# Attention and a gated feed-forward layer on one core: the output products of the last two token blocks in Strassen's form

## The chip, the core and the metric

The kernel runs on one core of a Trainium2 chip. The core has five engines that run side by side, each through its own queue in order: PE (TensorE, the matmuls; its weight loads are shown apart as PEld), DVE (VectorE), ACT (ScalarE), POOL (GpSimd) and SP (SyncE, here only a DMA queue). Matmuls write to PSUM, eight banks of 128 partitions x 512 float32; DVE and ACT read it. The metric is the device time of one execution in microseconds (us), the median of several runs.

## The reference

```
scores = q @ k.T / 8 + bias[bucket(|i - j|), head]     # 8 sequences, 8 heads, 576 tokens, 64 wide
attn   = softmax(scores)
x      = (attn @ v), heads side by side                # 4608 tokens x 512
h      = x @ w_in                                      # 512 -> 2048
g      = h + sin(alpha * h)^2 / (alpha + 1e-9)
out    = g @ w_out                                     # 2048 -> 512, float32
```

The part that is changed is the last line, for 1024 of the 4608 tokens.

## The kernel before

All matmuls take float16 operands and add up in float32. The 4608 tokens are nine blocks of 512 (b = 0 to 8); the eight sequences of 576 tokens are stages t = 0 to 7. A stage has an exp phase (scores of sequence t, their exponentials on ACT, multiplication with the exponential of the bias on DVE near the diagonal, products with V on PE, normalisation on DVE), and then a sin phase: the input products of token block t, `plan_moe_in`, for 16 groups f of 128 hidden columns: four matmuls of 512 tokens into one of six PSUM banks ("h", banks 0 to 5), sin on ACT, the square on ACT or DVE, and the g of that group on DVE, which reads the bank a last time and frees it. The last stage, t = 7, has two blocks in its sin phase, 7 and 8. ACT changes its function table between the two phases.

The output products of block b, `plan_mo`, are four row blocks of 128 tokens (a = 0 to 3). Each is 16 matmuls, one per group f, with 128 tokens of g as weights and 512 columns of `w_out16` streaming, into one bank ("mo", banks 7 and 6); then a copy to SBUF by ACT or DVE, and one DMA of 128 x 512 float32 on the SP queue. The last row block, (8, 3), is cut in 384 and 128 columns. Output matmuls are marked `fill`: they are worked off wherever PE would have to wait, those of block t mostly in the exp phase of stage t + 1. Those of blocks 7 and 8 come after the input products of block 8, but for a few that fill in before.

The order of each engine's queue is made by a planner in the kernel (`Plan.run`) before anything is built: every step is a task with engines and estimated durations, what it depends on, a priority, and the buffers and banks that it takes; the planner puts the tasks on a simulated clock, always the one that can start first, by priority among those. That order is then written out, with semaphores. What an engine finds in its queue is therefore fixed: a step that waits holds up all that stands behind it.

Names that matter below: `gdone[(b, f)]` is the task that makes g of group f; `mo_last` chains all output matmuls in one sequence; `new_u()` and `new_outs()` take the next buffer of rings of two and five; a helper records every matmul, so all of them have one line (L458 before the change, L459 after it), and so have the plain copies (L538 on ACT, L540 on DVE). L1083 is g, L1069 the sin, L1076 and L1078 the square on ACT and DVE, L739 the bias multiplication, L708 the exponential, L953 and L954 the normalisation, L1141 the output DMA.

The heart of an output row block before:

```
for f in range(NF):
    full(m.v[:, 0 : c1 - c0], gcell[b].v[:, f, 128 * a : 128 * a + 128],
         w_out16[:, f, c0:c1], f == 0, f == NF - 1)
copy_on(e, o, m.v[:, 0 : c1 - c0])
nc.sync.dma_start(out=out[r0 : r0 + 128, c0:c1], in_=o)
```

Of the kernel before, what the change touches and what calls it, by code (L numbers as in the profile page):

```python
# [10 lines left out]
F16 = mybir.dt.float16  # L11
F32 = mybir.dt.float32
AF = mybir.ActivationFunctionType
ALU = mybir.AluOpType
# [6 lines left out]
def t_pe(n):  # L21
    return n / 2400.0 + 0.0025


def t_act(n):
    return n / 1200.0 + 0.052


def t_dve(n):
    return n / 960.0 + 0.07  # L30
# [4 lines left out]
LAT = {"PE": 0.2, "ACT": 0.18, "DVE": 0.18, "POOL": 0.2, "SP": 2.4}  # L35
NBUF = {"ut": 2, "u": 2, "g": 2, "s16": 3, "sq": 3, "outs": 5, "xn": 6}
PAIRS = ((0, 1), (2, 3), (4, 5))
BANKS = {"h": (0, 1, 2, 3, 4, 5), "av": (6, 7), "mo": (7, 6)}


class Task:
# [212 lines left out]
CP_PRI = 0  # L254
# [16 lines left out]
def kernel(  # L271
# [74 lines left out]


    xT = sgl.tile([128, NP, XN], F16, name="xT")


    natx = tp.tile([128, NF * DM], F16, name="natx", tag="g", bufs=2)
# [13 lines left out]
    def new_u():  # L365
        return tp.tile([128, 2, 9, 512], F16, name="u", tag="u", bufs=NBUF["u"])
# [18 lines left out]
    def bank(b, n=1):  # L385
        k = b.banks[0]
        return pb[:, k, :] if n == 1 else pb[:, k : k + n, :]
# [66 lines left out]
        eng.memset(vhs[i][64:128, :, VC + D : VC + D + 1], 1.0)  # L454
        eng.memset(vs[i][:, :, :, D : D + 1], 1.0)

    def full(out, lhsT, rhs, start, stop):
        nc.tensor.matmul(out=out, lhsT=lhsT, rhs=rhs, start=start, stop=stop)  # L458

    def warm(n, k=7):  # L460
        for _ in range(n):
# [74 lines left out]
    def copy_on(e, o, i):  # L536
        if e == "ACT":
            nc.scalar.activation(out=o, in_=i, func=AF.Copy)  # L538
        else:
            k_of(e).tensor_copy(out=o, in_=i)  # L540
# [263 lines left out]
    def plan_att(t, gates, gate):  # L804

        us = [(Cell(), Buf("u")) for _ in range(2)]
        tb, done = Buf("ut"), {}
        tails[t] = tb, done
        A = [(p, "A", c) for p in range(NP) for c in range(4)]
        runs = (A[0:3], [(0, "C", 0)], A[3:6], A[6:9], A[9:12], [(2, "C", 0)], A[12:15],  # L810
                A[15:] + [(0, "B", 0), (2, "B", 0)], [(0, "X", 0)])
        bases = [PB + 700 * i for i in range(len(runs))]
        exps, head, seen = [], [], set()
        for i, units in enumerate(runs):
            base = bases[i]
            made, deps, new, use = [], list(gates), [], []
            fresh = []
            for k, (p, kind, c) in enumerate(units):
                g = p // 2
                u, ub = us[g] if kind in "AC" else (None, tb)  # L820
                if ub not in new + use:
                    if ub in seen:
                        use.append(ub)
                    else:
                        new.append(ub)
                        seen.add(ub)
                        if u:
                            fresh.append(u)
                made.append(plan_unit(t, p, kind, c, u, ub, done, gate, base + 30 * k))
                if t < 2:  # L830
                    for pp in {"A": (p,), "C": (p, p + 1), "B": (p, p + 1), "X": range(NP)}[kind]:
                        deps += tr[(t, pp, 0)][1 if kind in "CX" else 0] + tr[(t, pp, 1)][0]
            tl = plan_tail(t - 1, base) if i == 0 and t > 1 else None

            def run(e, i=i, made=made, tl=tl, fresh=fresh):
                if i == 0:
                    plan.in_qk, plan.used = True, 0
                    plan.quota = QUOTA1 if t == 1 else QUOTA
                for u in fresh:
# [14 lines left out]
            m.offs = ([d] if tl else []) + [0.0] * len(new) + [  # L854
                0.1 + 0.2185 * k - GUARD[x[1]] * (k > 1) for k, x in enumerate(units)]
            m.marks = [(x[1], o) for x, o in zip(made, ends)] + ([(tl[4], d + D_TAIL)] if tl else [])
            head = [m]
            exps += [x[3] for x in made]
        for p in range(NP):
            plan_av(t, [(p, 128 * i) for i in range(3)], *us[p // 2], done, bases[(2, 3, 5, 7)[p]],  # L860
                    p < (2, NP - 1)[t > 1])
        for g in range(2):
            ps = [[2 * g, 2 * g + 1]] if g == 0 or t > 1 else [[2], [3]]
            for x in ps:
                plan_av(t, [(p, 384) for p in x], *us[g], done,
                        bases[(4, 7)[g]] + 50 if g == 0 or t == 1 else PB + AV_LATE, g == 0 or t > 1)
        return exps
# [248 lines left out]
    def plan_mo(b, a):  # L1116

        for c0, c1 in ((0, 384), (384, DM)) if (b, a) == (T, 3) else ((0, DM),):
            mb, ob, m = Buf("mo"), Buf("outs"), Cell()
            n = c1 - c0  # L1120
            for f in range(NF):

                def mm(e, f=f, m=m, mb=mb, c0=c0, c1=c1):
                    if f == 0:
                        m.v = bank(mb)
                    full(
                        m.v[:, 0 : c1 - c0], gcell[b].v[:, f, 128 * a : 128 * a + 128],
                        w_out16[:, f, c0:c1], f == 0, f == NF - 1,
                    )

                mo_last[:] = [plan.add({"PE": t_pe(n)}, mm, mo_last[:] + [gdone[(b, f)]],
                                       500000000 + 4 * b + a, nb=T_WO[f // 4] if b == 0 else 0.0,
                                       new=[mb] if f == 0 else [],
                                       use=[gbuf[b]] if f == 0 else [gbuf[b], mb])]
                mo_last[0].fill = True

            def cp(e, m=m, c0=c0, c1=c1):
                o = new_outs()[:, 0 : c1 - c0]
                copy_on(e, o, m.v[:, 0 : c1 - c0])
                r0 = 512 * b + 128 * a  # L1140
                nc.sync.dma_start(out=out[r0 : r0 + 128, c0:c1], in_=o)  # L1141

            y = plan.add({"DVE": t_dve(n), "ACT": t_act(n)}, cp, mo_last[:], CP_PRI,
                         new=[ob], use=[mb])
            y.s_only = True

    def set_table(name):
        nc.scalar.preload_act_table_set(name)  # L1148
        plan.sin = name == SIN_SET

    PB = 0
# [6 lines left out]
    for t in range(T):  # L1158
        PB = 1000000 * t

        if t > 0:
            gate = [plan.add({"ACT": D_TBL}, lambda e: set_table(EXP_SET), sins, PB)]
        exps = []
        for p in range(NP - 1) if t == 0 else ():
            for kq in range(2):
                tr[(0, p + 1, kq)] = plan_tr(0, p + 1, kq, (150, 650, 5)[p], T_PAIR[p][kq])
        if t == 0:
            for g in range(2):
                exps += plan_att0(g, pe_gate, gate)
        else:  # L1170
            exps += plan_att(t, pe_gate, gate)
            if t == 1:
                exps += plan_late(PB + LATE, gate)
        if t == 0:
            for p in range(NP):
                for kq in range(2):
                    tr[(1, p, kq)] = plan_tr(1, p, kq, 10085 + 20 * p, T_TR1[kq])
            plan.add({"POOL": 5.0}, lambda e: stage_kq(2), [], 10090,
                     after=lds + [tr[(1, p, 0)][1][0] for p in range(NP)])

        def swap(e, t=t):
            set_table(SIN_SET)
        def turn_in(e, t=t):
            load_kqT(t + 1)
            load_kt(t + 1)

        tbl = [plan.add({"ACT": D_TBL}, swap, exps, PB)]
        if 1 <= t < T - 1:
            plan.add({"SP": 5.5}, turn_in, [], PB + 9000, after=tbl + [
                x for tt, _, _, x in xdone if tt == t and "SP" in x.engs])  # L1190
        if t == T - 1:
            tail_alone(t, PB + 10015)
        sins = []
        for b in [t] if t < T - 1 else [t, t + 1]:
            m, s_ = plan_moe_in(b, tbl)
            sins += s_
        pe_gate = [m]
        for b in [t] if t < T - 1 else [t, t + 1]:
            for a in range(4):
                plan_mo(b, a)  # L1200
    plan.run(T_START)


# [28 lines left out]
```

## Time and profile before

| | |
|---|---|
| median of 3 runs | 372.43 us (372.38 to 375.17) |
| span of the profiled execution, first to last instruction | 370.2 us |
| PE busy | 362.5 us, 98% |
| ACT busy | 316.8 us, 86% |
| DVE busy | 257.0 us, 69% |
| output matmuls with 512 columns | 592 |

The runs are timed without a profile; of the profiled execution only the span is known, and 2.2 us lie between it and the median. Times in the timeline and in the chain are microseconds from the span's start. A row of the timeline has start, length, engine, line, operation, what it writes and reads, how many instructions are merged in it, and in brackets how long the engine had stood idle and what it waited for. A row of the groups has line, engine, operation, shapes and count, then busy time, the mean length of one in ns, and the idle time ahead of them. The page divides the span into 40 equal slices and gives the busy share of each in tenths.

### The profile page before, as it was taken

Reading aid. Unit: us, or ns where it says so; the run is one execution under the profiler, and the core shown is the slowest. Engines: PE = TensorE matmul, PEld = TensorE weight load, DVE = VectorE, ACT = ScalarE, POOL = GpSimd, SP = SyncE. Lnnn points to the kernel's source line nnn. Section 1 sums busy time; section 2 is a strip of 40 time slices with the busy share of each in tenths; the row PEclk is TensorE's granted clock in tenths of the full one; section 3 lists DMA queues with packets and bytes.
Section 4 is the critical chain, followed back from the end, with each engine's and each line's share of the span. In section 5 each row is a group of like instructions: output and inputs, shape, how many; then the busy total and the mean of one; then the engine's idle time right before and its main releaser. Section 6 shows DMA issues by size and latency. Waiting matters only on the chain.

```text
span 370.2 us, 8922 instructions
## 1 busy us (share of the span) xinstructions
PE 362.5 (98%) x3576; PEld 195.7 (53%) x3576; DVE 257.0 (69%) x557; ACT 316.8 (86%) x433; POOL 92.0 (25%) x133
## 2 busy tenths in 40 slices
PE   7989999999999999999999999999999999999996
PEld 3564545644555446774554456445566455444443
DVE  4797957588677967696759776886769665979000
ACT  3998999899997999899979998999979997999111
POOL 7487450073000900073005600280005000000000
PEclk9999999999999999999999999999999999999999
DMA  9989999699525993399719991699259121000212
GB/s 169 199 160 205 201 163 147 132 90 141 99 58 109 122 161 71 86 134 143 119 48 146 141 145 53 135 115 171 68 105 104 61 69 37 7 28 4 84 60 86
DMA packets 149114, 40.49 MB, mean 109 GB/s; under 512 B 137080, under 2 KB 143568, under 8 KB 149072
## 3 DMA queue, kind: packets, MB, share of 16 engines
q0 software_dynamic: 96032, 17.67, 59.1%
q1 hardware_dynamic: 52864, 22.16, 25.4%
q8 instruction: 28, 0.46, 0.5%
q10 hardware_dynamic: 176, 0.09, 0.1%
q14 instruction: 14, 0.11, 0.1%
HBM read 37.73 MB, written 16.56 MB: 147 GB/s over the span
## 4 chain that ended last, share of the span: by engine, by line
PE 91%; ACT 5%; issue 1%; DVE 1%; ACTq 0%
PE pb L458 90%; ACT u L708 2%; ACT s L1069 1%; ACT sq L1076 1%; DVE u L739 1%; PE pb L1025 1%; PE pb L557 0%; ACT kT L538 0%; ACT qT L538 0%; DVE qT L540 0%; PE pb L551 0%; DVE xn L954 0%; DVE zz L509 0%; ACT outs L538 0%; DVE rd L953 0%
## 5 line engine op out<-in xcount | busy, mean ns | idle before, releaser
L708 ACT ACTIVATE u<-pb 128x1024 f16<-128x1024 f32 (+1 forms) x146 | 137.4, 1016 | 8.2 <-PE pb L458 6.7
L458 PE MATMUL pb<-w_out,g 128*128 128x512 f16 (+2 forms) x592 | 138.8, 374 | 0.0
L458 PE MATMUL pb<-xT,w_in 128*128 128x512 f16 (+4 forms) x704 | 127.6, 340 | 0.0
L1083 DVE SCALAR_TENSOR_TENSOR g<-sq,inv_a,pb 128x512 f16<-128x512 f16 x144 | 101.0, 743 | 7.1 <-ACT sq L1076 2.8
L1069 ACT ACTIVATE s<-pb,alphaT 128x512 f16<-128x512 f32 x144 | 93.0, 694 | 11.6 <-PE pb L458 10.8
L458 PEld LDWEIGHTS <-w_in 128*128 128x128 f16 x704 | 64.8, 98 | 57.4 <-issue 0.3
L739 DVE TENSOR_TENSOR u<-u,m2r 128x512 f16<-128x512 f16 (+1 forms) x128 | 62.2, 491 | 35.7 <-ACT u L708 32.5
L458 PEld LDWEIGHTS <-g 128*128 128x128 f16 x592 | 53.9, 98 | 59.9 <-issue 5.0
L458 PEld LDWEIGHTS <-u 128*128 128x128 f16 x1152 | 43.4, 97 | 10.4 <-issue 4.6
L403 POOL COPY kt<-kT 64x256 f16<-64x256 f16 x12 | 5.0, 421 | 171.2 <-DMA kT<-staged_k 86.3
L1076 ACT ACTIVATE sq<-s 128x512 f16<-128x512 f16 x71 | 44.4, 638 | 1.2 <-DVE g L1083 0.3
L458 PE MATMUL pb<-v,u 128*128 128x65 f16 x1024 | 44.1, 193 | 0.3 <-DVE u L739 0.3
L458 PE MATMUL pb<-qT,kT 64*128 64x64 f16 (+1 forms) x512 | 41.5, 285 | 1.5 <-ACT u L708 0.7
L1078 DVE TENSOR_TENSOR sq<-s 128x512 f16<-128x512 f16 x73 | 30.2, 423 | 12.4 <-ACT s L1069 11.5
L954 DVE TENSOR_TENSOR xn<-pb,rd 128x256 f16<-128x256 f32 (+2 forms) x59 | 28.5, 483 | 2.0
L458 PEld LDWEIGHTS <-kT 64*128 64x128 f16 x512 | 16.3, 94 | 22.9 <-issue 15.9
L458 PE MATMUL pb<-vh,u 128*128 128x130 f16 x128 | 28.2, 221 | 0.0
L408 POOL DMA_DIRECT2D v<-in_v_dram x28 | 24.8, 897 | 4.5 <-DMA nat<-in_k_dram 2.7
L538 ACT ACTIVATE outs<-pb 128x512 f32<-128x512 f32 (+2 forms) x12 | 6.8, 569 | 19.9 <-PE pb L458 19.9
L953 DVE RECIPROCAL rd<-pb 128x4 f32<-128x4 f32 (+2 forms) x59 | 10.9, 185 | 12.4 <-PE pb L458 12.3
L1148 ACT ACT_TABLE_LOAD x15 | 19.2, 1283 | 0.3
L540 DVE COPY outs<-pb 128x512 f32<-128x512 f32 x25 | 17.1, 685 | 3.2 <-PE pb L458 3.2
(75 smaller groups left out, 186.6 us busy)
## 6 DMA issues: line engine op xcount, KB each, us to landing
out_dram<-outs SPq DMA_DIRECT2D x35, 256.0 KB, 2.7
v<-in_v_dram POOLq DMA_DIRECT2D x28, 128.0 KB, 4.9
staged_k<-in_k_dram POOLq DMA_DIRECT2D x6, 576.0 KB, 9.1
staged_q<-in_q_dram POOLq DMA_DIRECT2D x6, 576.0 KB, 12.5
w_in<-in_moe_w_in_dram POOLq DMA_DIRECT2D x4, 512.0 KB, 8.7
w_out<-in_moe_w_out_dram POOLq DMA_DIRECT2D x4, 512.0 KB, 15.1
w_out<-in_v_dram SPq DMA_DIRECT2D x6, 128.0 KB, 6.2
xT<-xn SPq DMA_TRANSPOSE x47, 2.8
```

The costliest lines, as they stand in the source:

```text
L408: nc.gpsimd.dma_start(out=vs[t % 2][:, c, :, 0:D], in_=vp[128 * c : 128 * c + 128],)
L458: nc.tensor.matmul(out=out, lhsT=lhsT, rhs=rhs, start=start, stop=stop)
L540: k_of(e).tensor_copy(out=o, in_=i)
L708: nc.scalar.activation(out=o, in_=x, func=AF.Exp, scale=0.125)
L739: nc.vector.tensor_tensor(out=io, in0=io, in1=m2[:, 2 * p : 2 * p + 2, x0 : x0 + hi - lo], op=ALU.mult)
L953: nc.vector.reciprocal(out=r, in_=x[:, :, :, D])
L954: nc.vector.tensor_tensor(out=xn[:, 0:n].rearrange("p c (z d) -> p c z d", z=2), in0=x[:, :, :, 0:D], in1=r.unsqueeze(3).to_broadcast([128 ...
L1069: nc.scalar.activation(out=s16.v, in_=h.v, func=AF.Sin, scale=alphaT[:, f : f + 1])
L1076: nc.scalar.activation(out=sq.v, in_=s16.v, func=AF.Square)
L1078: k_of(e).tensor_tensor(out=sq.v, in0=s16.v, in1=s16.v, op=ALU.mult)
L1083: nc.vector.scalar_tensor_tensor(out=gcell[b].v[:, f, :], in0=sq.v, scalar=inv_a[:, f : f + 1], in1=h.v, op0=ALU.mult, op1=ALU.add,)
L1148: nc.scalar.preload_act_table_set(name)
```

## The change

For blocks 7 and 8 the output product is computed for pieces of 256 tokens, as a 2 x 2 block product in Strassen's form (Winograd's variant). A piece (b, a), a = 0 or 2, has the two row blocks a and a + 1 of g, each halved into hidden columns 0 to 1023 and 1024 to 2047 (eight groups f each), and `w_out16` halved both ways. Instead of eight half products (one row block x 1024 x 256 columns, eight matmuls of 256 columns each) seven are made:

- Four sums of blocks of g per piece, float16, 128 x 1024 each, on DVE, into a buffer of the ring "u" that the attention used before (`pre`).
- Four sums of blocks of `w_out16`, once, into a new tile `wsum`, as 16 DVE instructions of 128 x 512: four in each exp phase of stages 2 to 5 (`plan_wsum`), each tied to one of the exponentials of its stage.
- Products "a" (three of them add up in one bank, which is copied out to SBUF after the first, the second and the third), "c", "b", "d", "e"; the four quarters of the output are then a bank plus one of those copies, added by DVE (`add`), each with a DMA of its own of 128 x 256. The last product of the last piece is cut in two of 128 columns.
- The products of a piece start only when all 16 g's of its block are done (`gall`); before, each matmul waited for its own group alone. They may use all eight banks ("st").

The diff, cut to its core:

```diff
-BANKS = {"h": (0, 1, 2, 3, 4, 5), "av": (6, 7), "mo": (7, 6)}
+BANKS = {"h": (0, 1, 2, 3, 4, 5), "av": (6, 7), "mo": (7, 6), "st": (7, 6, 0, 1, 2, 3, 4, 5)}
...
+    wsum = sgl.tile([128, 4, NF // 2, DM // 2], F16, name="wsum")
...
+    def plan_wsum(t, deps):
+        n = DM // 2
+        quad = [[w_out16[:, NF // 2 * i : NF // 2 * i + NF // 2, n * j : n * j + n] for j in range(2)]
+                for i in range(2)]
+        todo = (
+            (0, quad[0][1], quad[0][0]),
+            (1, quad[1][1], wsum[:, 0]),
+            (2, quad[1][1], quad[0][1]),
+            (3, quad[1][0], wsum[:, 1]),
+        )
+        k, x, y = todo[t]
+        for i, d in enumerate(deps):
+            r = slice(2 * i, 2 * i + 2)
+            def sm(e, k=k, x=x, y=y, r=r):
+                nc.vector.tensor_tensor(out=wsum[:, k, r], in0=x[:, r], in1=y[:, r], op=ALU.subtract)
+            wdone.append(plan.add({"DVE": 0.36}, sm, [d] + wdone[-4:], PB + 9500))
...
+    def plan_half(b, a):
+        H2, n = NF // 2, DM // 2
...
+        def pre(k, x, y, op, deps):
+            def sm(e):
+                if k == 0:
+                    u.v = new_u()
+                nc.vector.tensor_tensor(out=sums(k), in0=x(), in1=y(), op=op)
+            return plan.add({"DVE": 0.63}, sm, deps, base - 100, new=[ub] if k == 0 else [],
+                            use=[gbuf[b]] if k == 0 else [ub, gbuf[b]])
+        s1 = pre(0, lambda: act(1, 0), lambda: act(1, 1), ALU.add, gall)
+        s2 = pre(1, lambda: sums(0), lambda: act(0, 0), ALU.subtract, [s1])
+        s3 = pre(2, lambda: act(0, 0), lambda: act(1, 0), ALU.subtract, [s1])
+        s4 = pre(3, lambda: act(0, 1), lambda: sums(1), ALU.subtract, [s2])
+        def prod(k, x, w, first, deps, c0=0, c1=n):
+            for f in range(H2):
+                def mm(e, f=f):
+                    if f == 0 and first:
+                        bv[k].v = bank(bk[k])
+                    full(bv[k].v[:, c0:c1], x()[:, f], w()[:, f, c0:c1], first and f == 0, f == H2 - 1, not first)
+                mo_last[:] = [plan.add({"PE": t_pe(c1 - c0)}, mm, mo_last[:] + deps, base,
+                                       new=[bk[k]] if f == 0 and first else [],
+                                       use=([] if f == 0 and first else [bk[k]]) + [ub, gbuf[b]])]
+                mo_last[0].fill = True
+            return mo_last[0]
...
+        p = prod("a", lambda: act(0, 0), wq(0, 0), True, gall)
+        x = keep("a", 0, p)
+        p = prod("c", lambda: act(0, 1), wq(1, 0), True, gall)
+        c11 = add("c", 0, (o1[0], 0, 0), [p, x], o1[1], True)
+        p = prod("a", lambda: sums(1), ws(1), False, [x, s2] + wdone)
+        y = keep("a", 1, p)
+        p = prod("b", lambda: sums(0), ws(0), True, [s1] + wdone)
+        w = add("b", 1, None, [p, y])
+        p = prod("a", lambda: sums(2), ws(2), False, [y, s3] + wdone)
+        z = keep("a", 2, p)
+        add("b", 2, (o2[0], 1, 1), [p, z, w], o2[1], True)
+        p = prod("d", lambda: sums(3), wq(1, 1), True, [s4])
+        add("d", 3, (o1[0], 0, 1), [p, w, c11], o1[1])
+        cuts = ((0, n // 2), (n // 2, n)) if (b, a) == (T, 2) else ((0, n),)
+        for (c0, c1), k in zip(cuts, "ef"):
+            p = prod(k, lambda: act(1, 1), ws(3), True, [], c0, c1)
+            add(k, 2, (o2[0], 1, 0), [p, z], o2[1], False, c0, c1)
...
+            if 2 <= t < 6:
+                plan_wsum(t - 2, exps[3:15:3])
...
-        for b in [t] if t < T - 1 else [t, t + 1]:
+        if t < T - 1:
             for a in range(4):
-                plan_mo(b, a)
+                plan_mo(t, a)
+        else:
+            for b in (t, t + 1):
+                for a in (0, 2):
+                    plan_half(b, a)
```

`act(i, j)` is half j of row block a + i of g, `wq` and `ws` are quarters of `w_out16` and of `wsum`, `keep` is a copy of a bank of 128 x 256 to SBUF (ACT or DVE, as the planner finds), `add` a DVE addition of a bank and such a copy.

More of the change, by code (lines that the diff above doesn't have):

```diff
@@ L455, in clear, with full @@
         eng.memset(vs[i][:, :, :, D : D + 1], 1.0)
-    def full(out, lhsT, rhs, start, stop):
-        nc.tensor.matmul(out=out, lhsT=lhsT, rhs=rhs, start=start, stop=stop)
+    def full(out, lhsT, rhs, start, stop, go_on=False):
+        nc.tensor.matmul(out=out, lhsT=lhsT, rhs=rhs, start=start, stop=stop, skip_group_check=go_on)
     def warm(n, k=7):
@@ new lines, with act, sums, part @@
+    wdone = []
+    def plan_half(b, a):
+        H2, n = NF // 2, DM // 2
+        u, ub = Cell(), Buf("u")
+        bk = {k: Buf("st") for k in "abcdef"}
+        bv = {k: Cell() for k in "abcdef"}
+        o1, o2 = (Cell(), Buf("outs")), (Cell(), Buf("outs"))
+        r0 = 512 * b + 128 * a
+        gall = [gdone[(b, f)] for f in range(NF)]
+        base = 500000000 + 4 * b + a
+        def act(i, j):
+            return gcell[b].v[:, H2 * j : H2 * j + H2, 128 * (a + i) : 128 * (a + i) + 128]
+        def sums(k):
+            return u.v.rearrange("p y k q -> p (y k q)")[:, 1024 * k : 1024 * k + 1024].rearrange(
+                "p (f t) -> p f t", f=H2)
+        def part(k):
+            w = u.v.rearrange("p y k q -> p (y k q)")[:, 4096:6144].bitcast(F32)
+            return w[:, n * k : n * k + n]
+        def pre(k, x, y, op, deps):
[20 more added lines that the diff above has]
+            return mo_last[0]
+        def wq(i, j):
+            return lambda: w_out16[:, H2 * i : H2 * i + H2, n * j : n * j + n]
+        def ws(k):
+            return lambda: wsum[:, k]
+        def keep(k, j, dep):
+            def cp(e):
+                copy_on(e, part(j), bv[k].v[:, 0:n])
+            return plan.add({"ACT": t_act(n), "DVE": t_dve(n)}, cp, [dep], CP_PRI, use=[bk[k], ub])
+        def add(k, j, to, deps, put=None, first=False, c0=0, c1=n):
+            def ad(e):
+                if to is None:
+                    nc.vector.tensor_tensor(out=part(3), in0=bv[k].v[:, 0:n], in1=part(j), op=ALU.add)
+                    return
+                cell, i, h = to
+                if first:
+                    cell.v = new_outs()
+                o = cell.v[:, n * h + c0 : n * h + c1]
+                nc.vector.tensor_tensor(out=o, in0=bv[k].v[:, c0:c1], in1=part(j)[:, c0:c1], op=ALU.add)
+                r = r0 + 128 * i
+                nc.sync.dma_start(out=out[r : r + 128, n * h + c0 : n * h + c1], in_=o)
+            ob = [put] if put else []
+            return plan.add({"DVE": t_dve(c1 - c0) + 0.03}, ad, deps, CP_PRI,
+                            new=ob if first else [], use=[bk[k], ub] + ([] if first else ob))
+        p = prod("a", lambda: act(0, 0), wq(0, 0), True, gall)
[15 more added lines that the diff above has]
+            add(k, 2, (o2[0], 1, 0), [p, z], o2[1], False, c0, c1)
```

## The prediction

> **What bounds the kernel now.** I read the page first (busy shares, the span in slices), then the chain of waits, then the timeline of the end.
>
> ```profile
> span 370.2 us, 8922 instructions
> ...
> PE 362.5 (98%) x3576; PEld 195.7 (53%) x3576; DVE 257.0 (69%) x557; ACT 316.8 (86%) x433; POOL 92.0 (25%) x133
> ...
> DVE  4797957588677967696759776886769665979000
> ACT  3998999899997999899979998999979997999111
> ...
> PEclk9999999999999999999999999999999999999999
> ```
>
> ```profile
> 269.51 39.54 PE pb L458 x444
> 309.05 0.17 PE pb L1025 x3
> 309.22 57.62 PE pb L458 x328
> 366.84 0.03 ACTq L538
> ...
> 366.91 0.28 ACT outs L538
> ```
>
> PE is busy 98% at the full granted clock, and the chain stays on PE from the start of token block 7's stage to the last output copy: columns that PE need not stream come off the end, as long as no other engine makes it wait. The last three slices show DVE empty and ACT at a tenth: there is room for the new sums and copies. A busy PE need not be a PE at its peak, so I check that on the output products themselves, by the copies that follow each 16-matmul group:
>
> ```profile
> 340.07 26.75 PE L458 MATMUL pb<-w_out,g 128*128 128x512 f16 x139
> 342.64 0.60 ACT L538 ACTIVATE outs<-pb 128x512 f32<-128x512 f32 x1 [0.27 <-PE pb L458]
> 363.41 0.60 ACT L538 ACTIVATE outs<-pb 128x512 f32<-128x512 f32 x1 [2.86 <-PE pb L458]
> 366.01 0.49 ACT L538 ACTIVATE outs<-pb 128x384 f32<-128x384 f32 x1 [2.00 <-PE pb L458]
> 366.91 0.28 ACT L538 ACTIVATE outs<-pb 128x128 f32<-128x128 f32 x1 [0.40 <-PE pb L458]
> ```
>
> From 342.64 to 363.41 lie six groups: 20.77 / 96 = 216.3 ns a matmul of 512 columns. The last row block is cut in 384 and 128 columns: (366.01 - 363.41) / 16 = 162.5 ns and (366.91 - 366.01) / 16 = 56.3 ns. So the price is proportional to the columns plus about 3 ns, down to 128, with a new weight load for every matmul. Check: of the 139 matmuls 107 are full, 107 x 0.2163 + 2.60 + 0.90 = 26.6 us against 26.75 shown.
>
> **The change, part by part.** *PE stream.* A product of 256 columns isn't in the trace; the line through 128 and 384 gives 109.4 ns. Before: 112 x 0.2163 + 2.60 + 0.90 = 27.73 us for both blocks. After: four pieces of 7 products x 8 matmuls, the last product in two column halves: 216 x 0.1094 + 16 x 0.0563 = 24.53 us. Gain 3.20 us, all on the path. That is 88 matmuls, and 88 weight loads, more:
>
> ```profile
> L458 PEld LDWEIGHTS <-g 128*128 128x128 f16 x160 | 14.9, 98 | 15.8
> ```
>
> No row hides a load behind a shorter product than the 56.3 ns above, and those ran without a gap although one load is listed at 98 ns: cost taken nothing. Against this stands the Trainium skill, TensorE: Matmul & The Clock Gate, section Back-to-back issue gap: in streams of load and matmul it gives about 81 ns a matmul at 128 columns and 131 at 512, so that half the columns cost well over half. An estimate by a line between that page's figures is 98 ns at 256, which would make the change about 4 us slower; the trace's 56.3 and 216.3 ns differ from it at both ends, and I keep the trace.
>
> *Operand sums, 16 on DVE, and where they bite.* Rows for the price:
>
> ```profile
> L1078 DVE TENSOR_TENSOR sq<-s 128x512 f16<-128x512 f16 x73 | 30.2, 423 | 12.4 <-ACT s L1069 11.5
> L739 DVE TENSOR_TENSOR u<-u,m2r 128x768 f16<-128x768 f16 x64 | 35.5, 556 | 8.7 <-ACT u L708 7.8
> L954 DVE TENSOR_TENSOR xn<-pb,rd 128x384 f16<-128x384 f32 x28 | 15.6, 558 | 1.0
> L954 DVE TENSOR_TENSOR xn<-pb,rd 128x256 f16<-128x256 f32 x29 | 12.3, 424 | 1.0
> L954 DVE TENSOR_TENSOR xn<-pb,rd 128x128 f16<-128x128 f32 x2 | 0.6, 292 | 0.1
> ```
>
> 256 more f16 columns cost 133 ns, so 1024 take 0.69 us; at the f32 rows' rate (134 ns per 128) it would be 0.424 + 6 x 0.134 = 1.23 us. I take 0.69: the operands are f16 like those of the first two rows. In the changed kernel's built order five sums (four of piece (7,0), one of (7,2)) stand between block 7's last g and block 8's first g. That g releases the bank of block 8's seventh input product, and PE waits for it:
>
> ```profile
> 326.89 0.75 DVE L1083 SCALAR_TENSOR_TENSOR g<-sq,inv_a,pb 128x512 f16<-128x512 f16 x1
> 327.56 0.97 DVE L1078 TENSOR_TENSOR sq<-s 128x512 f16<-128x512 f16 x2
> 329.71 1.89 PE L458 MATMUL pb<-w_out,g 128*128 128x512 f16 x8
> 330.63 4.70 DVE L1083 SCALAR_TENSOR_TENSOR g<-sq,inv_a,pb 128x512 f16<-128x512 f16 x7 [2.10 <-PE pb L458]
> 331.44 8.80 PE L458 MATMUL pb<-xT,w_in 128*128 128x512 f16 x40
> ```
>
> DVE has a hole of 2.10 us here. After: one square instead of two ends near 328.05, five sums 3.45 us to 331.50, g another 0.74 to 332.24. PE meanwhile runs three full matmuls and 15 of the new ones from 329.71: 0.65 + 1.64, to 332.00. So PE waits 0.3 us (0 if sums follow each other closer than their listed length, 2.9 us at the slow rate). After that DVE gives a g every (4.70 - 0.74) / 6 = 0.66 us and PE needs one every 4 x 0.216 = 0.86, so the lag shrinks. Behind the waiting DVE stand squares and g's whose s and sq buffers ACT needs; ACT then lags with them, by the same third of a microsecond, and six banks cover that.
>
> Later sums have room: a piece is 56 x 0.1094 = 6.1 us of PE against 4 x 0.69 + 5 x 0.42 = 4.9 us of DVE. The adds of (7,0) stand in DVE's queue among block 8's last g's and wait for products that PE runs only after that block's input products; queued behind them are g's whose banks PE wants two to five products (1.7 to 4.4 us) later. Nothing.
>
> *Copies and adds.* Two of three copies per piece must land before PE accumulates into the bank again. Between the 0.28 and 0.49 us rows of 128 and 384 columns, each is about 0.4 us on an idle ACT, behind one product of 8 x 0.109 = 0.87 us. Cost nothing; without that cover 0.4 x 8 = 3.2 us, the whole gain. The last add replaces the 0.28 us copy by 0.29 (the 128-column row): +0.01.
>
> *Output DMAs*, 17 in place of 9 for these blocks:
>
> ```profile
> L1141 SPq DMA_DIRECT2D out_dram<-outs x37: 332/337/563, 53.1 to 367.2; - x37
> out_dram<-outs SPq DMA_DIRECT2D x3, 256.0 KB, 2.0
> out_dram<-outs SPq DMA_DIRECT2D x1, 64.0 KB, 1.6
> ```
>
> 0.34 us of SP each, never closer than the 0.45 us of the last half product: nothing. The last one has its 64 KB as before.
>
> *Weight sums*, 16 of 0.42 us, four in each exp phase of stages 2 to 5. In stage 3:
>
> ```profile
> 134.21 0.43 DVE L739 TENSOR_TENSOR u<-u,m2r 128x512 f16<-128x512 f16 x1 [0.89 <-ACT u L708]
> 138.03 0.69 DVE L540 COPY outs<-pb 128x512 f32<-128x512 f32 x1 [0.21 <-PE pb L458]
> 138.64 0.88 DVE L739 TENSOR_TENSOR u<-u,m2r 128x512 f16<-128x512 f16 x2
> 139.55 0.23 PE L458 MATMUL pb<-vh,u 128*128 128x130 f16 x1
> 140.28 0.56 DVE L739 TENSOR_TENSOR u<-u,m2r 128x768 f16<-128x768 f16 x1 [0.76 <-ACT u L708]
> 144.14 0.43 DVE L739 TENSOR_TENSOR u<-u,m2r 128x512 f16<-128x512 f16 x1 [0.76 <-ACT u L708]
> ```
>
> By the built order the first and third sum fall into the holes of 0.89 and 0.76 us, the second is half taken up by the 0.21 us, the fourth by the last 0.76. The tightest reader is the product at 139.55: its multiply is the first of the pair at 138.64, done at about 139.07, and 0.23 later after the change, still ahead. PE's order there moves only by one or two output matmuls ahead of a product with V, which fills rather than idles. I take 0.1 us in all; the bound is 16 x 0.44 = 7.0.
>
> Sum: -3.20 + 0.30 + 0.01 + 0.10 = -2.8 us, span 367.4. The profiled execution's span is 370.2, the median of the runs 372.43; I leave the 2.2 us around the span as it is: **369.6 us**, 0.75% less. A measurement of this kernel tells about 1% from no change, so that counts as no change.
>
> **Rivals.** (a) *More than the stream*: if PE doesn't wait at block 8 (3.20), the smaller pieces ahead of the last DMA shorten its end by up to the 0.4 us between the landings of 256 and 64 KB, and the denser order of stages 2 to 5 gives 0.2, it is 3.8 us less: 368.6. For it: every cost above may be nothing; against it: the last DMA is no smaller. 0.20.
>
> (b) *The sums run at the f32 rows' rate*: a wait of 2.9 us at block 8, then 4 x 1.23 + 5 x 0.42 = 7.0 us of DVE a piece against 6.1 of PE, 0.9 for each of three more pieces: -3.2 + 2.9 + 2.7 + 0.1 = +2.5, 374.9. Against it: every f16 row above is at the faster rate. 0.08.
>
> (c) *Slower: the weight sums land on the path.* In the exp phases ACT and PE are both full, and if each sum delays a multiply for which PE waits, nothing gives that back: 16 x 0.44 - 2.9 = +4.1, 376.6. It decides from 0.18 us a sum. For it: products start within half a microsecond of their multiply; against it: the holes. 0.08.
>
> (d) *Slower: the saving isn't there*, since a half-wide matmul costs nearly as much as a wide one (weight loads setting the pace; the direction of the skill's rule above). At the 162.5 ns of the 384 row: 216 x 0.1625 + 0.9 = 36.0, +8.3 us, 380.7. It turns at (27.73 - 0.9) / 216 = 124 ns. Against it: 56.3 ns at 128 columns. 0.04.
>
> **How the numbers follow.** Forecast 0.60, (a) 0.20, (b) 0.08, (c) 0.08, (d) 0.04. Faster by over 1% (below 368.7) is (a): 0.20. Slower by over 1% (above 376.15) is (c) and (d): 0.12. Within 1%: 0.68. The range of the forecast goes from no wait at all (369.2) to a wait of 2.9 us (372.2); with (a) and a little scatter below it, 368.2 to 372.4, it leaves out (b), (c) and (d), 0.20.
>
> **What would show it.** After: copies of the first product of successive pieces 6.1 us apart (109 ns a matmul); block 8's first g ending near 332.2, where it ended at 331.4 (330.63 + 0.75); 16 sums near 0.69 us; the end of stage 5 (the input products of block 6) not later than before; the last add's start 2.9 us earlier than 366.91. The prediction is wrong if the 256-column product is above 115 ns, if PE shows holes between pieces, or if stages 2 to 5 are over 0.2 us longer each.

## The result, and the profile after

| | before | after |
|---|---|---|
| median of 20 runs each | 372.35 us (371.76 to 376.34) | 369.65 us (369.00 to 373.62) |
| span of the profiled execution | 370.2 us | 367.2 us |

The ratio is 0.9931, with a 95% interval of 0.9910 to 0.9952: a gain of 2.7 us, which is real by the interval and below the 1% that the prediction called a change. Forecast were 369.6 us.

First the page of the kernel after: the span, the busy times, and three rows of the span in 40 slices. The same rows of the kernel before stand in the prediction.

```profile
span 367.2 us, 9181 instructions
...
PE 359.4 (98%) x3664; PEld 204.4 (56%) x3664; DVE 279.2 (76%) x609; ACT 316.5 (86%) x437; POOL 91.7 (25%) x133
...
DVE  4797957678777967697759777796769675999972
ACT  3998999899997999799989999799979997999411
...
PEclk9999999999999999999999999999999999999999
```

PE has 88 matmuls more (3664 against 3576) and is busy 3.1 us less. DVE works 22.2 us more, and its last three slices, empty before, stand at 9, 7 and 2 tenths: the work moved from the engine that sets the end to one that had stood idle there. DVE pays seven times what PE saves.

The chain of waits of the kernel after, at its end (start, length, engine and line):

```profile
309.17 54.53 PE pb L459 x417
363.70 0.02 issue
363.72 0.29 DVE outs L1246
```

It has the shape of before: PE from the start of block 7's stage (309.17, before 309.22) to one last operation that empties a bank. The stretch on PE is 54.53 us long instead of 57.62. These 3.09 us are nearly all of the 3.19 us by which the last operation starts earlier; of the span, 3.0 us remain. Nothing was won or lost ahead of 309 us: that point differs by 0.05 us.

### The profile page after: what moved, and what is told of

Its sections match the earlier page's. It is cut to its first block, busy times and chain, and to the rows that moved or that the text cites. A ratio compares the mean times of both kernels' runs of the same rounds, so it can differ in the third digit from the quotient of the medians.

```text
span 367.2 us, 9181 instructions
## 1 busy us (share of the span) xinstructions
PE 359.4 (98%) x3664; PEld 204.4 (56%) x3664; DVE 279.2 (76%) x609; ACT 316.5 (86%) x437; POOL 91.7 (25%) x133
## 4 chain that ended last, share of the span: by engine, by line
PE 90%; ACT 6%; DVE 2%; issue 1%; ACTq 0%
PE pb L459 89%; ACT u L709 3%; ACT s L1070 1%; DVE u L740 1%; ACT sq L1077 1%; PE pb L1026 1%; PE pb L558 0%; ACT kT L539 0%; ACT qT L539 0%; PE pb L552 0%; DVE qT L541 0%; DVE xn L955 0%; DVE outs L1246 0%; DVE zz L510 0%; DVE u L726 0%
## 5 line engine op out<-in xcount | busy, mean ns | idle before, releaser
L459 PE MATMUL pb<-w_out,g 128*128 128x512 f16 (+1 forms) x512 | 119.0, 366 | 0.0
L459 PEld LDWEIGHTS <-g 128*128 128x128 f16 x552 | 50.1, 98 | 47.4 <-issue 6.2
L459 PEld LDWEIGHTS <-u 128*128 128x128 f16 x1280 | 56.2, 97 | 11.3 <-issue 3.6
L1077 ACT ACTIVATE sq<-s 128x512 f16<-128x512 f16 x73 | 45.5, 637 | 0.9
L1079 DVE TENSOR_TENSOR sq<-s 128x512 f16<-128x512 f16 x71 | 29.3, 421 | 12.5 <-ACT s L1070 11.5
L539 ACT ACTIVATE u<-pb 128x256 f32<-128x256 f32 x12 | 4.6, 384 | 15.8 <-PE pb L459 15.8
```

The lines of the kernel that those rows point to most:

```text
L1077: nc.scalar.activation(out=sq.v, in_=s16.v, func=AF.Square)
L1079: k_of(e).tensor_tensor(out=sq.v, in0=s16.v, in1=s16.v, op=ALU.mult)
```

## The experiments

Two questions were open after the result. Is the gain the stream, 3.2 us, with nothing given back, or more than that with something lost elsewhere? And are the covers named in the prediction (DVE's hole ahead of block 8's first g, the product behind which a copy hides, the holes in the exp phases) what makes the rest cost nothing, or would it cost nothing anyway? Experiments 1 to 6 each change one of these; 7 and 8 try two further steps. All medians below stand beside runs of the kernel before on the same chip (372.55 us for experiments 1 to 4, 372.27 for 5 to 8), and each ratio is to that kernel. The changed kernel was not run again beside them: distances to it are to its 369.65 us above, where the kernel before had 372.35. Between runs the start of the program varies by a microsecond (the sine table load of the last stage lies between 307.2 and 308.5 us where nothing ahead of it is changed), so within a trace I compare lengths, not times of day.

**1. Half-wide products without Strassen's form.** The kernel before, with the output products of blocks 7 and 8 in two halves of 256 columns: the columns are the same, the matmuls and weight loads nearly twice as many (272 for 144, since the last row block had been cut already).

```diff
-        for c0, c1 in ((0, 384), (384, DM)) if (b, a) == (T, 3) else ((0, DM),):
+        if b < T - 1:
+            cuts = ((0, DM),)
+        elif (b, a) == (T, 3):
+            cuts = ((0, 256), (256, 384), (384, DM))
+        else:
+            cuts = ((0, 256), (256, DM))
+        for c0, c1 in cuts:
```

> The kernel before, with the output products of blocks 7 and 8 cut into column halves of 256 (eight half products per 256 tokens, no sums, no Strassen form). Theory 1 (a matmul costs its columns plus about 3 ns, and the gain is the seventh of eight that isn't streamed): 128 more matmuls cost about 3 ns each, 0.3 us more than before, 372.7, with 256-column matmuls near 109 ns. Rival 2 (half-wide matmuls are cheaper or dearer than half, so that part of the 2.7 us of the change comes from the width itself): at 98 ns it would be 2.6 us less than before, 369.8; at 124 ns 4 us more, 376.4.

Measured: 372.67 us against 372.55, ratio 1.0016 (0.9984 to 1.0048). The timeline of this kernel has the copies behind two successive groups of 16 matmuls of 256 columns:

```profile
358.80 0.38 ACT L538 ACTIVATE outs<-pb 128x256 f32<-128x256 f32 x1 [1.36 <-PE pb L458]
360.55 0.38 ACT L538 ACTIVATE outs<-pb 128x256 f32<-128x256 f32 x1 [1.36 <-PE pb L458]
```

1.75 us for 16 is 109.4 ns a matmul, as the line through 128 and 384 columns gave. A half-wide matmul costs half of 216.3 to within 1.3 ns, so rival (d) falls. The cut itself gains or loses nothing that the medians can tell (by the interval, between 0.6 us less and 1.8 us more).

**2. Six products instead of seven.** The product "d" is left out of every piece, and its addition takes the bank of "b" in its place, so that one quarter of each of these output blocks is not the reference's.

```diff
-        p = prod("d", lambda: sums(3), wq(1, 1), True, [s4])
-        add("d", 3, (o1[0], 0, 1), [p, w, c11], o1[1])
+        add("b", 3, (o1[0], 0, 1), [s4, w, c11], o1[1])
```

> The changed kernel without product d (its add takes the bank of product b instead, so one quarter of the output of blocks 7 and 8 is something else; the sum for d is still made). Theory 1 (PE alone sets the pace of the four pieces): 4 x 8 x 0.109 = 3.5 us less than the changed kernel, 366.15, pieces 5.25 us apart. Rival 3 (sums, copies and adds help to set the pace): pieces stay near 6.1 us apart, and less than 2 us are gained.

Measured: 366.39 us, ratio 0.9839 (0.9820 to 0.9857), 3.26 less than the changed kernel. In its timeline the copies of the first product of successive pieces:

```profile
345.97 0.38 ACT L539 ACTIVATE u<-pb 128x256 f32<-128x256 f32 x1 [1.36 <-PE pb L459]
351.26 0.38 ACT L539 ACTIVATE u<-pb 128x256 f32<-128x256 f32 x1 [1.41 <-PE pb L459]
356.50 0.38 ACT L539 ACTIVATE u<-pb 128x256 f32<-128x256 f32 x1 [1.41 <-PE pb L459]
```

5.24 us a piece instead of 6.11: a product of 0.87 us, 8 x 0.109, is worth its whole length in each piece (four are 3.5 us; the medians show 3.26, and the trace shows the last output DMA issued 0.3 us later behind its addition than in the changed kernel). PE is still the bound of the pieces when another seventh of the stream goes, so the sums, copies and adds are not.

**3. Every sum of g twice.** This takes away DVE's hole ahead of block 8's first g.

```diff
-                nc.vector.tensor_tensor(out=sums(k), in0=x(), in1=y(), op=op)
+                for _ in range(2):
+                    nc.vector.tensor_tensor(out=sums(k), in0=x(), in1=y(), op=op)
```

> The changed kernel with every sum of blocks of g written twice (16 more DVE instructions of 128 x 1024). Theory 1: the reserve at block 8's first g is 0.34 us (g ends at 331.60, PE comes to it at 331.94); five more sums of 0.60 us delay that g by 3.0, so PE waits 2.7 there, and nowhere else (later sums have about 2 us or more of reserve): 372.3. Rival 3 (DVE paces the pieces): 2.7 and about 0.8 more for each of three pieces, 374.8. Rival 4 (the sums have room everywhere): 369.7.

Measured: 376.26 us, ratio 1.0105 (1.0069 to 1.0141). The place was right, the size was not: 6.6 us more than the changed kernel (6.4 by the spans of the profiled executions, 373.6 against 367.2). The timeline of this kernel at the place, a g and the matmuls that wait for it:

```profile
332.03 1.41 DVE L1199 TENSOR_TENSOR u<-g 128x1024 f16<-128x1024 f16 x2
333.36 1.41 DVE L1199 TENSOR_TENSOR u<-g,u 128x1024 f16<-128x1024 f16 x2
334.69 3.37 DVE L1084 SCALAR_TENSOR_TENSOR g<-sq,inv_a,pb 128x512 f16<-128x512 f16 x5
335.49 10.22 PE L459 MATMUL pb<-xT,w_in 128*128 128x512 f16 x40 [3.17 <-DVE g L1084]
```

Its stretches, with the columns start and end, length, busy time and count of PE, PEld, DVE, ACT and POOL, then the granted clock, the DMA share and GB/s:

```profile
332.00:335.40 3.40, 0.31 (x3) 0.13 (x2) 3.33 (x7) 0.00 (x0) 0.00 (x0) 0.94 0.24 82
335.40:338.60 3.20, 3.12 (x8) 1.08 (x8) 2.67 (x5) 2.41 (x5) 0.00 (x0) 0.53 0.01 3
345.60:368.00 22.40, 22.40 (x210) 19.98 (x209) 21.95 (x42) 6.21 (x15) 0.00 (x0) 1.00 0.16 54
```

Four things are in these 6.4 us. PE reaches the 40 input matmuls 3.55 us later (335.49 against 331.94): it waits 3.17 us for the bank, its trace starts 0.2 us later, and the rest is that a matmul's listed end lies behind the point at which the next one could start. Then its granted clock is 0.53 for 3.2 us, and the 40 input matmuls take 10.22 us instead of 8.80: 1.42. DVE, busy for 21.95 of 22.40 us by the last row, ends its last addition (at 369.65 us) 1.00 us after PE's last matmul, where it was 0.32 in the changed kernel: 0.68. And the last output DMA is issued another microsecond later, where it was 0.21 (experiment 7 returns to this queue): 0.80.

```profile
370.66 0.41 SPq L1249 DMA_DIRECT2D out_dram<-outs  x1
```

In the last of the three stretches PE has no gap: the pieces themselves hide twice the sums, but for what DVE and the DMA queue lag at the very end. So the limit lies where the prediction looked for it, and the changed kernel doesn't reach it. The expectation missed because it counted the wait alone, at the spacing of the single sums, 0.60 us. A sum that writes the same output again starts 0.73 us after the first (1.41 for two, less the 0.68 of one), which makes a pair 1.33 us long (333.36 - 332.03) instead of 1.20.

**4. No weight sums.** The 16 sums of `w_out16` are not made, and the products take a quarter of `w_out16` in their place, so blocks 7 and 8 of the output are not the reference's.

```diff
             def sm(e, k=k, x=x, y=y, r=r):
-                nc.vector.tensor_tensor(out=wsum[:, k, r], in0=x[:, r], in1=y[:, r], op=ALU.subtract)
+                pass
...
-            return lambda: wsum[:, k]
+            return wq(k % 2, k // 2)
```

> The changed kernel without the 16 sums of blocks of w_out: the products that used them take a quarter of w_out itself (another result), the plan is the same. Theory 1: they cost nothing, within 0.1 us: 369.65, and the sin phase of stage 7 begins at 307.5 as in both kernels. Rival 5 (they cost something that the changed order of stages 2 to 5 gives back): stages 2 to 5 are shorter by up to 0.2 us each, 368.9.

Measured: 369.51 us, ratio 0.9932 (0.9908 to 0.9955), where the changed kernel has 369.65: 0.14 us, less than the medians can tell. The traces tell more: from ACT's table load ahead of stage 2's exponentials to the one ahead of stage 7's sines it is 218.83 us here, 218.82 in the changed kernel and 218.76 in the kernel before. So the weight sums cost nothing that can be measured.

**5. Copies without cover.** The three products of bank "a" follow each other, so that PE has nothing else while the bank is copied.

```diff
         x = keep("a", 0, p)
-        p = prod("c", lambda: act(0, 1), wq(1, 0), True, gall)
-        c11 = add("c", 0, (o1[0], 0, 0), [p, x], o1[1], True)
         p = prod("a", lambda: sums(1), ws(1), False, [x, s2] + wdone)
         y = keep("a", 1, p)
-        p = prod("b", lambda: sums(0), ws(0), True, [s1] + wdone)
-        w = add("b", 1, None, [p, y])
         p = prod("a", lambda: sums(2), ws(2), False, [y, s3] + wdone)
         z = keep("a", 2, p)
+        p = prod("c", lambda: act(0, 1), wq(1, 0), True, gall)
+        c11 = add("c", 0, (o1[0], 0, 0), [p, x], o1[1], True)
+        p = prod("b", lambda: sums(0), ws(0), True, [s1] + wdone)
+        w = add("b", 1, None, [p, y])
```

> The changed kernel with the three products of bank a in succession, so that PE has to wait for the copy of that bank each time (in the first piece the second of them still falls behind block 8's input products). Theory 1 (the copies cost nothing only because a product of 0.87 us lies between): from a product's end to the copy's end pass 0.20 + 0.38 us and a little to PE's next start, 0.66 us, seven times: 4.6 us more, 374.3. Rival 3 (copies and adds set the pace anyway): under 1 us more.

Measured: 374.78 us, ratio 1.0054 (1.0031 to 1.0076): 5.1 us more than the changed kernel, and slower than before. From its timeline, one piece:

```profile
354.50 0.38 ACT L539 ACTIVATE u<-pb 128x256 f32<-128x256 f32 x1 [4.03 <-PE pb L459]
354.94 1.03 PE L459 MATMUL pb<-wsum,u 128*128 128x256 f16 x8 [0.52 <-ACT u L539]
...
356.00 0.38 ACT L539 ACTIVATE u<-pb 128x256 f32<-128x256 f32 x1 [1.12 <-PE pb L459]
356.44 1.03 PE L459 MATMUL pb<-wsum,u 128*128 128x256 f16 x8 [0.47 <-ACT u L539]
...
361.93 0.38 ACT L539 ACTIVATE u<-pb 128x256 f32<-128x256 f32 x1 [4.03 <-PE pb L459]
```

The pieces are 7.43 us apart instead of 6.11, so each of the two uncovered copies costs 0.66. That is more than the copy's 0.38, and more than the 0.47 to 0.52 for which PE is shown idle: a product is listed with 1.03 us, but within a stream the next one starts 0.87 after it, and these 0.16 belong to the stop. The order of the products, with another product between two that use one bank, is thus worth more than the saving itself. The prediction had named this cover, and priced its loss at 3.2 us; it is 5.1 (8 x 0.66 would be 5.3).

**6. Every weight sum four times.** This takes away the holes in the exp phases.

```diff
-                nc.vector.tensor_tensor(out=wsum[:, k, r], in0=x[:, r], in1=y[:, r], op=ALU.subtract)
+                for _ in range(4):
+                    nc.vector.tensor_tensor(out=wsum[:, k, r], in0=x[:, r], in1=y[:, r], op=ALU.subtract)
```

> The changed kernel with each of the 16 sums of blocks of w_out written four times (12 more DVE instructions of 0.42 us in each exp phase of stages 2 to 5, DVE from 14.5 to some 19.7 us of 20). Theory 1 (single ones fall into holes of 0.76 to 0.89 us or are made up in the next one): three more in each place (1.3 us) exceed the holes, PE waits for multiplies and normalisations, and each of these stages grows by 0.5 to 1.5 us: 371.6 to 375.6. Rival 5 (DVE there has room as long as it is not full): 369.7.

Measured: 381.37 us, ratio 1.0228 (1.0174 to 1.0283), 11.7 more than the changed kernel and well over what was expected. The exp phases of stages 2 to 5 as stretches, between the two table loads of ACT (columns as above), stage 3 of the kernel before:

```profile
127.81:149.28 21.47, 21.47 (x283) 11.73 (x282) 14.54 (x35) 20.52 (x23) 2.60 (x2) 1.00 1.13 126
```

stage 3 of the kernel after:

```profile
127.57:149.00 21.43, 21.43 (x283) 11.68 (x282) 15.70 (x39) 20.52 (x22) 2.38 (x2) 1.00 1.12 124
```

and stage 3 with every weight sum four times:

```profile
130.46:154.86 24.40, 21.84 (x283) 11.67 (x282) 20.18 (x51) 20.52 (x22) 3.06 (x2) 1.00 1.03 111
```

Four single sums put 1.2 us more on DVE in a phase of 21.4, and PE stays without a gap. Sixteen put 5.6 us there (4.5 more than the four), and the phase grows by 2.9; the other three stages do the same (four phases of 97.2 us in all, 85.5 in the changed kernel), which is the whole 11.7. DVE is even then free for 4.2 of 24.4 us, so its share of busy time doesn't tell the limit. The timeline of this kernel, in stage 2, shows what does:

```profile
101.49 1.79 DVE L1166 TENSOR_TENSOR wsum<-w_out 128x512 f16<-128x512 f16 x4
103.89 0.56 DVE L955 TENSOR_TENSOR xn<-pb,rd 128x384 f16<-128x384 f32 x1
104.50 0.22 PE L459 MATMUL pb<-vh,u 128*128 128x130 f16 x1 [1.59 <-DVE xn L955]
```

Four sums in a row put off the bias multiplications and, behind them, a normalisation that frees a bank; PE stands 1.59 us for it. Rival (c) is thus a real mechanism: one sum at a time is free, a group of four in a row costs 0.73 us (11.7 / 16).

**7. One output DMA on another queue.** The DMA of the last half product but one goes out from ACT's queue, so that SP is free for the last.

```diff
-                nc.sync.dma_start(out=out[r : r + 128, n * h + c0 : n * h + c1], in_=o)
+                q = nc.scalar if (c0, c1) == (0, n // 2) else nc.sync
+                q.dma_start(out=out[r : r + 128, n * h + c0 : n * h + c1], in_=o)
```

> The changed kernel with the DMA of the last half product but one issued from ACT's queue instead of SP's. Theory 1: the last DMA of the kernel no longer stands behind that one's issue, it is issued right after its add, 0.2 us earlier (from 364.01 instead of 364.21), span 367.0, time 369.45. Rival: the end of the span is set by something else, no change.

Measured: 369.45 us, ratio 0.9901 (0.9867 to 0.9935). Its last operations, from the timeline:

```profile
364.60 0.37 ACTq L1249 DMA_DIRECT2D out_dram<-outs  x1
364.72 0.29 DVE L1246 TENSOR_TENSOR outs<-pb,u 128x128 f32<-128x128 f32 x1 [0.16 <-PE pb L459]
```

```profile
365.04 0.33 SPq L1249 DMA_DIRECT2D out_dram<-outs  x1
```

The last DMA is issued 0.03 us after the last addition ends (365.01). From the start of that addition to the end of the span (368.0 us) it is 3.28 us, where the changed kernel has 3.48. The 0.2 us are there in the trace; in the medians they can't be told from nothing. This kernel has the lowest median of all versions that give the reference's output, and isn't distinguishable from the changed kernel by its time.

**8. Block 6 in the same form.** The output products of block 6, which are worked off in the exp phase of stage 7, get seven half products too: the same saving a third time, but now among scores and exponentials. The sums and copies of that block have buffers of their own, and the number of output matmuls that the planner lets into that phase is doubled, since each is half as wide.

```diff
-        if t < T - 1:
+        if t == T - 2:
+            for a in (0, 2):
+                plan_half(t, a)
+        elif t < T - 1:
...
-                    plan.quota = QUOTA1 if t == 1 else QUOTA
+                    plan.quota = QUOTA1 if t == 1 else 2 * QUOTA if t == T - 1 else QUOTA
```

> The changed kernel with the output products of block 6 in the same form as well (worked off in the exp phase of stage 7, sums in buffers that are idle then, products in any free bank, the planner's quota of output matmuls in that phase doubled since they are half as wide). PE has 1.6 us less to stream. Theory 6 (the gain comes off the end only where ACT and DVE are idle): that exp phase has ACT busy for 19.2 of 20 us, DVE gets some 9 us more, and the products take banks from the scores: no gain, 369.5 to 372. Rival 7 (PE alone is the bound in every stage): 368.1.

Measured: 375.48 us, ratio 1.0082 (1.0056 to 1.0108), 5.8 more than the changed kernel, where the columns alone would have given 1.6 less. The exp phase of stage 7 as a stretch, in the changed kernel and then in this one:

```profile
286.00:307.50 21.50, 21.50 (x282) 11.73 (x281) 14.50 (x35) 20.52 (x23) 0.00 (x0) 1.00 0.23 68
```

```profile
286.20:317.10 30.90, 27.02 (x360) 19.52 (x359) 22.99 (x54) 21.80 (x26) 0.00 (x0) 0.94 0.20 58
```

30.9 us instead of 21.5, and no engine is full. Behind the phase it is 2.0 us shorter (54.4 against 56.5 us to the end of the last addition), since more of the output products lie ahead. ACT's own timeline in that phase:

```profile
293.15 5.68 ACT L710 ACTIVATE u<-pb 128x1024 f16<-128x1024 f32 x6 [0.34 <-PE pb L460]
302.44 0.38 ACT L540 ACTIVATE part<-pb 128x256 f32<-128x256 f32 x1 [3.61 <-PE pb L460]
304.40 0.38 ACT L540 ACTIVATE part<-pb 128x256 f32<-128x256 f32 x1 [1.57 <-PE pb L460]
306.14 0.38 ACT L540 ACTIVATE part<-pb 128x256 f32<-128x256 f32 x1 [1.36 <-PE pb L460]
307.56 7.44 ACT L710 ACTIVATE u<-pb 128x1024 f16<-128x1024 f32 x8 [1.04 <-PE pb L460]
```

ACT does no exponential between 298.8 and 307.6 us: PE runs seven microseconds of output products in one go, without scores. When the scores come, the products are nearly used up, and PE waits for ACT, mostly for 0.5 us at a time. In the changed kernel's phase, from the first exponentials on, output products fill the gaps in lots of one to ten full matmuls (at most 2.3 us); here they stand in a lump. A part of the 30.9 us is the clock. PE stands for 0.88 us at the start of the phase, and from 288 to 290 us its granted clock is 0.50:

```profile
286.72 0.37 PE L460 MATMUL pb<-qT,kT 64*128 64x512 f16 x1 [0.88 <-DVE g L1085]
```

```profile
288.00:290.00 2.00, 2.00 (x38) 1.32 (x35) 1.75 (x6) 2.00 (x3) 0.00 (x0) 0.50 0.00 0
```

The profiled execution is one of four out of ten with a mean granted clock of 0.995, and these took 376.05 to 376.91 us; the other six, at 1.00, took 374.44 to 375.54. So the clock is worth about one microsecond, and the loss is there without it.

Why the planner made this order (the banks that the new products hold, or the doubled quota) was not tried. The form pays where PE has nothing else to do, at the end; a version of this order with the products spread was not made.

## Why the prediction was right, point by point

**The stream: right.** The timeline of the kernel after shows the copies of the first product of successive pieces:

```profile
346.24 0.38 ACT L539 ACTIVATE u<-pb 128x256 f32<-128x256 f32 x1 [2.24 <-PE pb L459]
352.40 0.38 ACT L539 ACTIVATE u<-pb 128x256 f32<-128x256 f32 x1 [2.29 <-PE pb L459]
358.51 0.38 ACT L539 ACTIVATE u<-pb 128x256 f32<-128x256 f32 x1 [2.29 <-PE pb L459]
```

They are 6.16 and 6.11 us apart, forecast 6.1; 6.11 / 56 is 109.1 ns. Experiment 1 gives the same price without the change, experiment 2 gives it from another side. None of the prediction's three signs of being wrong is there: 109 ns lies below 115, PE has no hole between the pieces, and stages 2 to 5 together are 0.06 us longer. (Of the 592 output matmuls in the table ahead of the prediction, 560 have 512 columns, 16 have 384 and 16 have 128; the prediction's sum has them right.) The rule of the Trainium skill that was weighed against it (TensorE: Matmul & The Clock Gate, Back-to-back issue gap) gives 81 ns at 128 columns and 131 at 512 for streams of load and matmul; here such streams ran at 56.3, 109.1 to 109.4 and 216.3 ns for 128, 256 and 512. The measurement decides, and by it the rule doesn't hold for this kernel. (Worked out with a line between the two figures for all widths, the estimate that the prediction called about 4 us slower is 4.6.)

**The wait at block 8's first g, +0.30: mis-sized, it is 0.** The same view, at that place:

```profile
327.84 1.28 DVE L1198 TENSOR_TENSOR u<-g 128x1024 f16<-128x1024 f16 x2
329.05 0.68 DVE L1198 TENSOR_TENSOR u<-u,g 128x1024 f16<-128x1024 f16 x1
329.65 0.68 DVE L1198 TENSOR_TENSOR u<-g 128x1024 f16<-128x1024 f16 x1
329.66 2.45 PE L459 MATMUL pb<-w_out,g 128*128 128x512 f16 x18
330.25 0.68 DVE L1198 TENSOR_TENSOR u<-g,u 128x1024 f16<-128x1024 f16 x1
330.85 4.86 DVE L1084 SCALAR_TENSOR_TENSOR g<-sq,inv_a,pb 128x512 f16<-128x512 f16 x7
331.94 8.80 PE L459 MATMUL pb<-xT,w_in 128*128 128x512 f16 x40
```

Each sum has the listed length that was priced, 0.68 against 0.69, but the next starts 0.60 us after it: five take 3.0 us from 327.84 to 330.85, not 3.45, and they start 0.2 us earlier than assumed. That g ends at 331.60 (330.85 + 0.75), forecast 332.24. PE reaches the matmuls behind it at 331.94, as worked out (332.00), and runs on without a gap. A reserve of 0.34 us stood where a wait of 0.30 was forecast. The prediction had kept that case ("0 if sums follow each other closer than their listed length") and took the other end; its own two times, 332.24 and 332.00, are 0.24 apart, which it rounded up to 0.30. The Trainium skill, Vector Engine (DVE) Microarchitecture Reference, section Measured stream behaviour on trn2, has 1.04 ns a column for 32-bit data and some 75 ns an instruction after overlap; with the column's share halved for 16-bit data, as an estimate, that is 0.61 us for 1024 columns, and the trace's 0.60 agrees. Experiment 3 shows that the place was the right one to look at.

**The weight sums, +0.10: mis-sized, it is 0.** The stretches of stage 3 under experiment 6 show both kernels without a gap on PE; stages 4 and 5 are the same, and in stage 2 PE is idle for 0.10 us of 21.10. The table load of stage 7 stands at 307.52 us against 307.57. Experiment 4 confirms it. Experiment 6 shows that this cover has an end: DVE had 5.7 us free in stage 3's phase of the changed kernel, and 4.5 us more of sums already lengthened it by 3.0.

**The copies, covered: right**, and experiment 5 shows the cover as the cause. Its loss was priced too low, 0.4 us a copy instead of 0.66.

**The last addition, +0.01: right.** 0.29 us, against a copy of 0.28.

**The output DMAs, "nothing": this step was wrong, by +0.2.** The SP queue at the end of the kernel after, four issues and the last of them alone, from two windows of the timeline:

```profile
362.82 1.79 SPq L1248 DMA_DIRECT2D out_dram<-outs  x4
...
364.22 0.40 SPq L1248 DMA_DIRECT2D out_dram<-outs  x1
```

and the last issue of the kernel before:

```profile
367.21 0.33 SPq L1141 DMA_DIRECT2D out_dram<-outs  x1
```

Before, the last copy ended at 367.19 and its DMA was issued at 367.21. After, the last addition ends at 364.01, and its DMA is issued at 364.22: SP still had the three before it to issue, four in 1.79 us, some 0.45 each. The prediction compared a length of 0.34 us with a distance of 0.45 between the last two half products. It left out that two more DMAs of 256 columns are ready just ahead of them, so that the queue is already behind when the last come, and that an issue in a row takes up 0.45. Experiment 7 takes one of them away, and the 0.2 us with it.

So the mechanism, and the term that carries the sum, were right: -3.2 on PE's stream as forecast. The small terms were wrong and cancel in part: 0.4 us of small costs that weren't there, 0.2 that was overlooked. In the span that is 3.0 us less where 2.8 were forecast, in the medians 2.7; that the median came to 0.05 us from the forecast is luck. Of the rivals, (a) had its first condition, no wait at block 8, but the end of the last DMA moved the other way, and stages 2 to 5 gave nothing. For (b), every f16 sum ran at the faster rate. (c) and (d) fell as shown.

## What to carry to other kernels

Where one engine is busy to the end and the others are empty there, work can be bought off it at a bad rate of exchange (here 22 us of DVE for 3 of PE) as long as every piece of the bought work lands in a hole. The same seven-for-eight form gained 2.7 us at the end of the kernel and lost 5.8 in the one version that took it on into a phase where exponentials and products share PE. So price the saving by its columns, then look for the one place at which the new work stands ahead of something that PE waits for, and keep another product between two that need one bank.

## What the runs showed of the hardware

- DVE's listed lengths overlap: f16 additions of 128x1024 listed at 0.68 us start 0.60 us apart, but 0.73 when the second writes the same output again (experiment 3).
- A wait of PE can cost more than its length. After 3.17 us of idle the granted clock was 0.53 for the next 3.2 us, which added 1.4 (experiment 3). The Trainium skill, TensorE: Matmul & The Clock Gate, What's actually happening, has half the clock after an idle window of about 3.4 us. Experiment 3 comes near that, with a wait a little shorter. It doesn't explain experiment 8: there the clock fell to 0.50 although the longest stop was 0.88 us, with PE idle for 1.17 us of the 3.00 from 285 to 288. The waits of half a microsecond in experiment 5 left the clock at 1.00. How much idle time it takes isn't shown.
- A stop of PE for a copy of 0.38 us cost 0.66 us of the stream (experiment 5).
- DMA issues on SP that stood in a row went out some 0.45 us apart (four in 1.79 us, in the changed kernel), though one alone is listed at 0.33.
